# The routing steps of a fused attention, expert and SiLU kernel: the gates placed by hand, the compaction ahead of the numbers' table, pair 1's windows copied by VectorE

## The chip, the cores and the metric

The program runs on one core of a Trainium2 chip. The core has five engines with instruction streams of their own: TensorE (PE, matrix products; PEld is its weight load), VectorE (DVE), ScalarE (ACT), GpSimd (POOL) and SyncE (SP, which here only issues DMAs). Each takes its stream in order and waits on semaphores for the others. The metric is the device time of one execution in microseconds.

## The reference

Three stages follow each other on 3072 tokens of 512 numbers, all in fp32:

```python
# chunked attention: per chunk of 32 queries, 8 memory keys and a window of 56 keys
a = softmax(scale * q_c @ concat(mem_k, k_ctx).T);  x[c] = a @ concat(mem_v, v_ctx)
# top-1 mixture of 8 experts
logits = unit(x) @ unit(expert_emb).T / tau
e = argmax(logits);  gate = softmax(logits)[e]
y = gate * (relu(x @ w1[e]) @ w2[e])
# SiLU MLP
h = y @ w_in;  out = (h * sigmoid(h)) @ w_out
```

## The kernel before

Products are made in split form: an operand is cut into a rounded part and its remainder (`split`, lines 92 to 94: ScalarE rounds, VectorE subtracts), and `three` (lines 96 to 100) adds three products.

**Attention.** 16 pairs of heads, two units each. For a unit, `scores` (line 788) multiplies queries with the windows of keys in `kbuf`, VectorE takes the maximum (797) and subtracts it (800), ScalarE exponentiates (805), TensorE turns the result (811), and `values` (823) multiplies with the values. `windows` (lines 710 to 719) lays out a pair's keys: from the loaded block `kraw` it copies 56 overlapping columns for each of 12 chunks (716, the large copy) and the 8 memory columns (717, the small copy). Head 0's go by ScalarE, head 1's by VectorE for pair 0 and by GpSimd for the others. `kbuf` holds two pairs. Ahead of its first copy GpSimd zeroes buffers and makes the routing constants (lines 278 to 292). Per block of tokens `ranks` finds each token's expert and its place among that expert's tokens.

**Experts.** Tokens are gathered into slots that belong to one expert each: two leading slots of 256 tokens whose experts are found early (`pre[0]`, `pre[1]`), then up to 4 slots of 384 (`threes`) and up to 17 of 256 (`twos`). Each slot has 8 steps. In `step` (f), TensorE makes the first product of part f+1 (`first_mm`, tokens by `w1`) and then the second product of part f (`second_mm`, by `w2`). Between them the two weight parts for f+2 are split (`split_w`: `w1h`, `w1l`, then `v2h`, `v2l`), and SyncE fetches part f+5. ScalarE and VectorE split the hidden part too (183, 184: `hhs`, `hls`). In the last two steps of a slot the next slot's gathered rows are turned and split (`turn`, lines 171 and 93/94: `xhl`, `xll`).

**The routing work beside it.** The place of every token is worked out while the leading slots run. It is written as generators (`places`, `gates`, `names`, `compact`) in the list `pending`. `advance` takes the next pieces of the first generator at each point where it is called. A bare `yield` ends a piece; a `yield n` also holds the list until a call behind a block of products comes, n calls later at least. `places` ends in one-hot matrices: VectorE makes `ahf` (513), GpSimd and ScalarE scale it into `ah` (517, 518), and TensorE multiplies four groups of six (506) into the table of rows; `meta` makes the counts. `names` turns the table and stores it in `td` (546 to 550), `compact` makes for each output row the place where it lies (`rows_i`, lines 555 to 572), and `gates` makes the softmax weight of each token and stores it in `gd` (580 to 601). What is left at the end of step 6 of `pre[1]` is forced out there (`while pending`).

Of the kernel before, what the change touches and what calls it, by code (L numbers as in the profile page):

```python
# [13 lines left out]
I32 = mybir.dt.int32  # L14
# [8 lines left out]
P = 128  # L23
# [25 lines left out]
NA = 2 * N2  # L49
# [10 lines left out]
def tile_chunk_attention_top1_moe_silu_mlp(ctx, tc, qT, kT, vW, emb, tau, wm, wo, out, dbg=None):  # L60
    nc = tc.nc
    wo = wo.bitcast(I32)
    PE, ACT, DVE, POOL, SP = nc.tensor, nc.scalar, nc.vector, nc.gpsimd, nc.sync
# [10 lines left out]
    bank = [psum.tile([P, DM], F32, name=f"bank{i}") for i in range(8)]  # L74
# [33 lines left out]
    rp = rt.enter_context(tc.tile_pool(name="rp", bufs=1))  # L108
# [87 lines left out]
    def put(at, y, nt):  # L196
# [3 lines left out]
    pre = [  # L200
        Slot(2, 4, None, chosen_i[0:1, n:n + 1], lambda c, n=n: pre_i[:, 2 * n + c:2 * n + c + 1], lambda n=n: later.get("chosen", 0) > n)
        for n in range(2)
    ]
# [58 lines left out]
    shift = rp.tile([P, 1], F32, name="shift")  # L262
    lens, skip, cends, cfirst = (rp.tile([P, 2, NE], F32, name=n) for n in ("lens", "skip", "cends", "cfirst"))
    wideh = rp.tile([P, NTC, 2 * NE], F32, name="wideh")
    ahf = rp.tile([P, NT, NA], BF16, name="ahf")
    ah = rp.tile([P, NT, 2, NA], BF16, name="ah")
    ixs = rp.tile([P, NA + 3 * N3], F32, name="ixs")
# [213 lines left out]
    def places(home):  # L481

        yield from slots()
        sl = slice(LEAD, NT)
        DVE.tensor_scalar(two[:, sl], mv[:, sl, 0], e2, None, op0=ALU.is_equal)
        DVE.tensor_scalar(too[:, sl], mv[:, sl, 0], e3, None, op0=ALU.is_equal)
        yield
        DVE.tensor_tensor(two, two, too, op=ALU.add)
        part = [P, 3, NE, NT]
        DVE.tensor_tensor(hotf, hot.unsqueeze(1).to_broadcast(part), look.to_broadcast(part), op=ALU.mult)  # L490
        yield
        DVE.tensor_reduce(found, hotf.rearrange("p n e t -> p n t e"), axis=AX.X, op=ALU.add)
        yield
        DVE.tensor_tensor(found[:, 0], found[:, 0], ab[:, 0], op=ALU.is_gt)
        DVE.scalar_tensor_tensor(two, two, float(SLOT), ab[:, 0], op0=ALU.mult, op1=ALU.is_gt)
        yield
        DVE.tensor_tensor(found[:, 2], found[:, 2], found[:, 0], op=ALU.mult)
        DVE.tensor_tensor(ab[:, 0], ab[:, 0], found[:, 1], op=ALU.add)
        yield
        DVE.tensor_tensor(ab[:, 0], ab[:, 0], found[:, 2], op=ALU.add)  # L500
        yield
        DVE.scalar_tensor_tensor(ab[:, 0], two, -float(4 * N), ab[:, 0], op0=ALU.mult, op1=ALU.add)
        yield
        def products(c):
            for t in range(c * TPB, (c + 1) * TPB):
                PE.matmul(ix, lhsT=bh[:, t], rhs=ah[:, t], start=t == 0, stop=t == NT - 1)

        tables = meta()
        ix = home[:, 0:2 * NA].rearrange("p (r a) -> p r a", r=2)
        for c in range(NT // TPB):  # L510
            sl = slice(c * TPB, (c + 1) * TPB)
            part = [P, TPB, NA]
            DVE.tensor_tensor(
                ahf[:, sl], ab[:, 0, sl].unsqueeze(2).to_broadcast(part), tiles.to_broadcast(part), op=ALU.is_equal
            )
            yield
            POOL.tensor_tensor(ah[:, sl, 1], ahf[:, sl], count[:, sl].unsqueeze(2).to_broadcast(part), op=ALU.mult)
            ACT.activation(ah[:, sl, 0], ahf[:, sl], AF.Copy, scale=row)
            yield
            if c:  # L520
                yield 0
                products(c - 1)
        yield from tables
        yield LASTW
        products(c)
        yield
        DVE.tensor_scalar(ixp, ix[:, 1], float(P), None, op0=ALU.mult)
        DVE.tensor_scalar(here, countf[:, 0:N3 + 1], ends3[:, NE - 1:], None, op0=ALU.is_equal)
        yield
        DVE.tensor_tensor(ixs[:, 0:NA], ixp, ix[:, 0], op=ALU.add)  # L530
        yield
        DVE.tensor_copy(rows3_i, ixs[:, 0:3 * (N3 + 1)])
        later["placed"] = True
        flush()
        DVE.tensor_scalar(ixp, ixs[:, 0:NA], here[:, 0:1], None, op0=ALU.mult)
        yield
        for k in range(1, N3 + 1):
            out_ = rows2_i if k == N3 else ixp
            DVE.scalar_tensor_tensor(out_, ixs[:, 3 * k:3 * k + NA], here[:, k:k + 1], ixp, op0=ALU.mult, op1=ALU.add)
            yield  # L540

    def names():

        yield HOLD
        by_tile = bank[7][0:NA, 0:P]
        PE.transpose(by_tile, ixs[:, 0:NA], ident)
        yield
        names_t = wideh.rearrange("p t e -> p (t e)")[0:NA, 0:P].bitcast(I32)
        DVE.tensor_copy(names_t, by_tile)
        SP.dma_start(out=td.rearrange("(t p) o -> t (p o)", p=P), in_=names_t)  # L550
        yield

    def compact():

        DVE.tensor_tensor(lens[:, 0], rem, wide, op=ALU.min)
        yield
        DVE.tensor_tensor(lens[:, 1], rem, lens[:, 0], op=ALU.subtract)
        yield
        flat16 = lambda t: t.rearrange("p a e -> p (a e)")
        yield from starts(flat16(cfirst), flat16(lens), flat16(cends))  # L560
        DVE.tensor_tensor(skip[:, 0], row3, cfirst[:, 0], op=ALU.subtract)
        DVE.tensor_tensor(skip[:, 1], row2, cfirst[:, 1], op=ALU.subtract)
        yield
        part = [P, NTC, 2 * NE]
        across = lambda t: flat16(t).unsqueeze(1).to_broadcast(part)
        DVE.tensor_tensor(wideh, token[:, 0:NTC].to_broadcast(part), across(cfirst), op=ALU.is_ge)
        yield
        DVE.tensor_tensor(wideh, wideh, across(skip), op=ALU.mult)
        yield
        DVE.tensor_reduce(st[:, 0:NTC], wideh, axis=AX.X, op=ALU.max)  # L570
        yield
        DVE.tensor_tensor(rows_i, st[:, 0:NTC, 0], token[:, 0:NTC, 0], op=ALU.add)
        yield

    def gates():
        norm = ss.unsqueeze(2)
        while squares:
            yield
        yield HOLD
        ACT.activation(ss, ss, AF.Sqrt)  # L580
        yield HOLD
        DVE.tensor_scalar(ss, ss, 1e-6, None, op0=ALU.add)
        yield
        DVE.reciprocal(ss, ss)
        yield
        DVE.tensor_tensor(d, d, norm.to_broadcast(full), op=ALU.mult)
        yield HOLD
        ACT.activation(d, d, AF.Exp)
        yield HOLD
        DVE.tensor_reduce(gate, d, axis=AX.X, op=ALU.add)  # L590
        yield
        DVE.tensor_scalar(gate, gate, 1e-9, None, op0=ALU.add)
        yield
        DVE.reciprocal(gate, gate)
        yield HOLD
        by_tile = bank[7][0:NT, 0:P]
        PE.transpose(by_tile, gate, ident)
        yield
        gate_t = flat(seg)[0:NT, 0:P]
        DVE.tensor_copy(gate_t, by_tile)  # L600
        SP.dma_start(out=gd.rearrange("(t p) o -> t (p o)", p=P), in_=gate_t)
        yield

    pending = []
# [20 lines left out]
    duty, tail, early, mid = (defaultdict(list) for _ in range(4))  # L625
# [44 lines left out]
    def step(s, f):  # L670
        ahead_of(s, f)
        firsts(s, f)
        seconds(s, f)

    SPOTS, HOLD, RATE, LASTW, GP = (2, 6), 2, 2, 1, 2
# [7 lines left out]
    with ExitStack() as a:  # L683
# [26 lines left out]
        def windows(j, h, part):  # L710
            rows = slice(h * D, h * D + D)
            half = slice(part * (NCH // 2), (part + 1) * (NCH // 2))
            src, dst = kraw[j][rows], kbuf[j % 2][rows, h, half]
            copy = (POOL.tensor_copy if j else DVE.tensor_copy) if h else ACT.copy
            w = src[:, NMEM + half.start * CH:]
            copy(dst[:, :, NMEM:], bass.AP(tensor=w.tensor, offset=w.offset, ap=[w.ap[0], [CH, NCH // 2], [1, WIN]]))
            (POOL.tensor_copy if j > 2 else copy)(
                dst[:, :, 0:NMEM], src[:, 0:NMEM].unsqueeze(1).to_broadcast([D, NCH // 2, NMEM])
            )
# [233 lines left out]
        for i in range(1, NF - 2):  # L953
            ahead_of(pre[0], i)
            firsts(pre[0], i)
            if i == 1:
                logits2(NU - 1)
                pending.extend([places(bank[6]), gates(), names(), compact()])
            seconds(pre[0], i)
            for b, t in squares[:2]:  # L960
                square(b, t)
            del squares[:2]
# [21 lines left out]
        tail[key].append(lambda at=at: put(at, yfirst[0], 2))  # L984
    step(pre[0], NF - 2)
    step(pre[0], NF - 1)
    for f in range(NF):
        step(pre[1], f)
        if f == NF - 2:
            while pending:  # L990
                advance(pe=True)
# [320 lines left out]
```

## Time and profile before

| | |
|---|---|
| three runs | 1022.92, 1024.77, 1028.66 us; median 1024.77 |
| the profiled execution | 1027.44 us, its span 1025.7 us |
| granted TensorE clock, mean | 0.992 of full speed |
| TensorE busy | 978.3 us, 95% of the span |
| VectorE busy | 596.8 us, 58% |
| ScalarE busy | 462.5 us, 45% |
| GpSimd busy | 188.8 us, 18% |

The profile comes from one execution. Busy shares are means over the three stages: attention runs up to about 110 us, the leading slots to about 172, the other expert slots to about 470, and the SiLU MLP behind them. In a row with a bracket, the bracket gives the time that the engine stood idle ahead of the instruction and what released it.

### The profile page before, as it was taken

How to read it: one execution, taken by the hardware profiler on the slowest of the kernel's cores; microseconds unless marked ns; L12 is line 12 of the kernel's file. 1: busy time of each engine (PE TensorE's matmuls, PEld its weight loads, DVE VectorE, ACT ScalarE, POOL GpSimd, SP SyncE). 2: the span in 40 equal slices, each digit the busy share in tenths (PEclk: the TensorE clock that was granted, in tenths of full speed). 3: DMA queues.
4: the chain of work that ended last, by engine and by line, in shares of the span. 5: the costliest groups of instructions: out<-in, count | busy, mean ns of one | idle time of the engine just before them, and what ended most of it. 6: DMA issues, size and time to landing. Idle time of an engine off the chain costs nothing. (4 is left out here: it accounts for less than half of the span.)

```text
span 1025.7 us, 16830 instructions
## 1 busy us (share of the span) xinstructions
PE 978.3 (95%) x6366; PEld 823.4 (80%) x6366; DVE 596.8 (58%) x1191; ACT 462.5 (45%) x890; POOL 188.8 (18%) x259
## 2 busy tenths in 40 slices
PE   5988888999999999998999999999999999999997
PEld 4766677999888999997778888878887888788886
DVE  6778797677777888896899932422332232223221
ACT  7877655445467665663544423222321331233221
POOL 8355133011020000013130002140032005001001
PEclk9999999999999999999999999999999999999999
DMA  7987756566487887776242201020010002000001
GB/s 271 350 317 261 258 190 226 173 219 222 131 272 265 280 274 257 263 248 186 84 137 95 76 1 42 21 62 1 1 58 25 1 1 83 1 1 24 18 1 42
DMA packets 44212, 139.36 MB, mean 136 GB/s; under 512 B 6422, under 2 KB 6480, under 8 KB 44120
## 3 DMA queue, kind: packets, MB, share of 16 engines
q1 hardware_dynamic: 36632, 118.22, 33.6%
q0 software_dynamic: 7488, 19.95, 6.4%
q8 instruction: 53, 0.87, 0.3%
q14 instruction: 39, 0.32, 0.1%
HBM read 115.32 MB, written 22.84 MB: 135 GB/s over the span
## 5 line engine op out<-in xcount | busy, mean ns | idle before, releaser
L1174 DVE TENSOR_TENSOR sg<-bank,sg 128x512 f32<-128x512 f32 x96 | 66.3, 690 | 235.5 <-ACT sg L1169 230.0
L1169 ACT ACTIVATE sg<-bank 128x512 f32<-128x512 f32 x96 | 57.4, 598 | 272.4 <-PE bank L100 262.0
L98 PE MATMUL bank<-yh,w2bh 128*128 128x512 f32 x240 | 94.3, 393 | 0.0
L94 DVE TENSOR_TENSOR gl<-sg,gh 128x512 fp32r<-128x512 f32 x92 | 63.8, 693 | 51.8 <-ACT gh L93 48.1
L100 PE MATMUL bank<-yh,w2bl 128*128 128x512 f32 x240 | 93.6, 390 | 0.0
L99 PE MATMUL bank<-yl,w2bh 128*128 128x512 f32 x240 | 93.5, 390 | 0.0
L1197 POOL DMA_INDIRECT out_dram<-o,tok x20 | 20.2, 1008 | 387.9 <-DVE o L1194 347.8
L100 PE MATMUL bank<-w2bh,gl 128*128 128x512 f32 x224 | 87.4, 390 | 0.0
L98 PE MATMUL bank<-w2bh,gh 128*128 128x512 f32 x224 | 87.2, 389 | 0.0
L93 ACT CAST gh<-sg 128x512 fp32r<-128x512 f32 x92 | 57.0, 620 | 66.9 <-DVE sg L1174 64.6
L99 PE MATMUL bank<-w2bl,gh 128*128 128x512 f32 x224 | 87.2, 389 | 0.0
L183 ACT ACTIVATE hhl<-bank 128x256 fp32r<-128x256 f32 (+1 forms) x88 | 36.4, 413 | 99.3 <-PE bank L100 94.2
L98 PE MATMUL bank<-v2h,hhl 128*128 128x512 f32 x200 | 80.3, 401 | 0.0
L100 PE MATMUL bank<-v2h,hll 128*128 128x512 f32 x200 | 78.8, 394 | 0.0
L99 PE MATMUL bank<-v2l,hhl 128*128 128x512 f32 x200 | 78.3, 392 | 0.0
L94 DVE TENSOR_TENSOR w1l<-raw,w1h 128x512 fp32r<-128x512 f32 x106 | 72.9, 688 | 8.6 <-ACT w1h L93 4.9
L149 POOL DMA_INDIRECT xrowl<-xd,rows_i x28 | 30.9, 1103 | 241.4 <-PE bank L171 199.8
L94 DVE TENSOR_TENSOR v2l<-raw,v2h 128x512 fp32r<-128x512 f32 x106 | 73.0, 689 | 0.0
L184 DVE SCALAR_TENSOR_TENSOR hll<-bank,hhl 128x256 fp32r<-128x256 f32 (+1 forms) x88 | 40.4, 459 | 52.6 <-ACT hhl L183 51.1
L99 PE MATMUL bank<-xll,w1h 128*128 128x256 f32 (+1 forms) x224 | 68.7, 306 | 2.2 <-DVE xll L94 2.2
L98 PE MATMUL bank<-xhl,w1h 128*128 128x256 f32 (+1 forms) x224 | 68.9, 307 | 1.4 <-DVEq L1139 1.4
L100 PE MATMUL bank<-xhl,w1l 128*128 128x256 f32 (+1 forms) x224 | 68.7, 306 | 0.2 <-DVE w1l L94 0.2
(309 smaller groups left out, 2433.9 us busy)
## 6 DMA issues: line engine op xcount, KB each, us to landing
raw<-in_wm_dram SPq DMA_DIRECT2D x109, 512.0 KB
coded<-in_wo_dram SPq DMA_DIRECT2D x36, 512.0 KB
vbuf<-in_vW_dram SPq DMA_DIRECT2D x32, 390.0 KB
k<-in_kT_dram SPq DMA_DIRECT2D x16, 400.0 KB
q<-in_qT_dram SPq DMA_DIRECT2D x16, 384.0 KB
xd<-xb SPq DMA_DIRECT2D x8, 768.0 KB
ys<-ymore SPq DMA_DIRECT2D x8, 512.0 KB
ys<-yfirst SPq DMA_DIRECT2D x7, 512.0 KB
```

The source lines that it names most:

```text
L93: ACT.copy(hi, src)
L94: eng.tensor_tensor(lo, src, hi.bitcast(F32), op=ALU.subtract)
L98: PE.matmul(out, lhsT=lh, rhs=rh, start=start, stop=False)
L99: PE.matmul(out, lhsT=lh, rhs=rl, start=False, stop=False)
L100: PE.matmul(out, lhsT=ll, rhs=rh, start=False, stop=stop)
L149: POOL.indirect_dma_start(out=s.where["row"][:, c], out_offset=None, in_=xd[0:LEAD * P] if s in pre else xd, in_offset=IndirectOffsetOnAxi ...
L183: ACT.activation(hh, h, AF.Relu)
L184: DVE.scalar_tensor_tensor(hl, h, 0.0, hh.bitcast(F32), op0=ALU.max, op1=ALU.subtract)
L1169: ACT.activation(sg, h, AF.Sigmoid)
L1174: DVE.tensor_tensor(sg, h, sg, op=ALU.mult)
L1197: POOL.indirect_dma_start(out=out, out_offset=IndirectOffsetOnAxis(ap=tok_i[g][:, c:c + 1], axis=0), in_=o, in_offset=None,)
```

## The change

It has four parts. `gates` leaves the list `pending`; a helper `share` runs it up to its next hold, and five such calls are hung at the end of steps 0 to 4 of `pre[1]`. `compact` stands ahead of `names` in the list. `names` gets a tile of its own, `names_t`, where it used the memory of `wideh`, which `compact` fills. The first group of one-hot products is held for one more call (`yield 1`). And pair 1's windows of head 1 are copied by VectorE.

```diff
--- before.py
+++ after.py
@@ -262,6 +262,7 @@
     shift = rp.tile([P, 1], F32, name="shift")
     lens, skip, cends, cfirst = (rp.tile([P, 2, NE], F32, name=n) for n in ("lens", "skip", "cends", "cfirst"))
     wideh = rp.tile([P, NTC, 2 * NE], F32, name="wideh")
+    names_t = rp.tile([NA, P], I32, name="names_t")
     ahf = rp.tile([P, NT, NA], BF16, name="ahf")
     ah = rp.tile([P, NT, 2, NA], BF16, name="ah")
     ixs = rp.tile([P, NA + 3 * N3], F32, name="ixs")
@@ -518,7 +519,7 @@
             ACT.activation(ah[:, sl, 0], ahf[:, sl], AF.Copy, scale=row)
             yield
             if c:
-                yield 0
+                yield 1
                 products(c - 1)
         yield from tables
         yield LASTW
@@ -545,7 +546,6 @@
         by_tile = bank[7][0:NA, 0:P]
         PE.transpose(by_tile, ixs[:, 0:NA], ident)
         yield
-        names_t = wideh.rearrange("p t e -> p (t e)")[0:NA, 0:P].bitcast(I32)
         DVE.tensor_copy(names_t, by_tile)
         SP.dma_start(out=td.rearrange("(t p) o -> t (p o)", p=P), in_=names_t)
         yield
@@ -574,9 +574,6 @@
 
     def gates():
         norm = ss.unsqueeze(2)
-        while squares:
-            yield
-        yield HOLD
         ACT.activation(ss, ss, AF.Sqrt)
         yield HOLD
         DVE.tensor_scalar(ss, ss, 1e-6, None, op0=ALU.add)
@@ -711,7 +708,7 @@
             rows = slice(h * D, h * D + D)
             half = slice(part * (NCH // 2), (part + 1) * (NCH // 2))
             src, dst = kraw[j][rows], kbuf[j % 2][rows, h, half]
-            copy = (POOL.tensor_copy if j else DVE.tensor_copy) if h else ACT.copy
+            copy = (POOL.tensor_copy if j > 1 else DVE.tensor_copy) if h else ACT.copy
             w = src[:, NMEM + half.start * CH:]
             copy(dst[:, :, NMEM:], bass.AP(tensor=w.tensor, offset=w.offset, ap=[w.ap[0], [CH, NCH // 2], [1, WIN]]))
             (POOL.tensor_copy if j > 2 else copy)(
@@ -955,7 +952,7 @@
             firsts(pre[0], i)
             if i == 1:
                 logits2(NU - 1)
-                pending.extend([places(bank[6]), gates(), names(), compact()])
+                pending.extend([places(bank[6]), compact(), names()])
             seconds(pre[0], i)
             for b, t in squares[:2]:
                 square(b, t)
@@ -984,6 +981,15 @@
         tail[key].append(lambda at=at: put(at, yfirst[0], 2))
     step(pre[0], NF - 2)
     step(pre[0], NF - 1)
+    assert not squares
+    shares = gates()
+
+    def share():
+        while next(shares, HOLD) is None:
+            pass
+
+    for f in range(5):
+        tail[pre[1], f].append(share)
     for f in range(NF):
         step(pre[1], f)
         if f == NF - 2:
```

On VectorE at the start, before: the maxima and subtractions of units 0 and 1, and then the expert norms.

```order
L797 TENSOR_REDUCE mx_277<-bank_69 128x6
L800 TENSOR_TENSOR e_279<-bank_69,mx_277 128x3x2x64
L797 TENSOR_REDUCE mx_298<-bank_70 128x6
L800 TENSOR_TENSOR e_300<-bank_70,mx_298 128x3x2x64
L728 TENSOR_SCALAR en_209<-en_209 8x1
L729 TENSOR_TENSOR en_209<-en_209 8x1
L730 RECIPROCAL en_209<-en_209 8x1
L731 TENSOR_SCALAR e_208<-e_208,en_209 8x512
L797 TENSOR_REDUCE mx_334<-bank_69 128x6
```

And of the change, with the four copies in between:

```order
L794 TENSOR_REDUCE mx_278<-bank_69 128x6
L797 TENSOR_TENSOR e_280<-bank_69,mx_278 128x3x2x64
L713 COPY kbuf_205<-k_223 64x12x56
L714 COPY kbuf_205<-k_223 64x12x8
L794 TENSOR_REDUCE mx_299<-bank_70 128x6
L797 TENSOR_TENSOR e_301<-bank_70,mx_299 128x3x2x64
L725 TENSOR_SCALAR en_210<-en_210 8x1
L726 TENSOR_TENSOR en_210<-en_210 8x1
L727 RECIPROCAL en_210<-en_210 8x1
L728 TENSOR_SCALAR e_209<-e_209,en_210 8x512
L713 COPY kbuf_205<-k_223 64x12x56
L714 COPY kbuf_205<-k_223 64x12x8
```

The first pair of copies stands ahead of unit 1's maximum, the second ahead of unit 2's.

On VectorE in `pre[1]`, before, from the last piece of `places` on (539, the rows of the slots of 256); the first `w1l` behind it is the split for part 5:

```order
L539 SCALAR_TENSOR_TENSOR ixp<-ixs,here,ixp 128x34 x3
L539 SCALAR_TENSOR_TENSOR rows_i<-ixs,here,ixp 128x34
L94 TENSOR_TENSOR w1l_106<-raw_100,w1h_105 128x512
L94 TENSOR_TENSOR v2l_112<-raw_100,v2h_111 128x512
L184 SCALAR_TENSOR_TENSOR hls_116<-bank_71,hhs_115 128x256
```

And of the change:

```order
L540 SCALAR_TENSOR_TENSOR rows_i<-ixs,here,ixp 128x34
L555 TENSOR_TENSOR lens<-rem,wide 128x8
L557 TENSOR_TENSOR lens<-rem,lens 128x8
L403 SCALAR_TENSOR_TENSOR cends<-lens,countf 128x16
L405 TENSOR_TENSOR cfirst<-cends,lens 128x16
L561 TENSOR_TENSOR skip<-row_167,cfirst 128x8
L562 TENSOR_TENSOR skip<-row_168,cfirst 128x8
L566 TENSOR_TENSOR wideh<-token,cfirst 128x320
L568 TENSOR_TENSOR wideh<-wideh,skip 128x320
L570 TENSOR_REDUCE st<-wideh 128x20
L94 TENSOR_TENSOR w1l_106<-raw_100,w1h_105 128x512
L94 TENSOR_TENSOR v2l_112<-raw_100,v2h_111 128x512
```

Nine operations of the compaction now stand ahead of that `w1l`. Three of the gate's (`ss`, its reciprocal and `d`) have moved a step further up, ahead of the fourth `ahf`.

On TensorE at the end of step 6 of `pre[1]`, before: the last second product, the two turns of small tables, and the turn of the gathered rows (171).

```order
L100 MATMUL bank_74<-v2h_107,hls_116 128x512
L597 MATMUL bank_76<-ident,gate 24x128
L546 MATMUL bank_76<-ident,ixs 34x128
L171 MATMUL bank_69<-ident,xrowl 128x128 x3
L171 MATMUL bank_70<-ident,xrowl 128x128 x3
```

And of the change, around step 4, where the two turns now stand:

```order
L100 MATMUL bank_72<-xhs,w1l_106 128x256
L547 MATMUL bank_76<-ident,ixs 34x128
L98 MATMUL bank_73<-v2h_2365,hhs_115 128x512
L99 MATMUL bank_73<-v2l_2366,hhs_115 128x512
L100 MATMUL bank_73<-v2h_2365,hls_116 128x512
L98 MATMUL bank_74<-v2h_2365,hhs_115 128x512
L99 MATMUL bank_74<-v2l_2366,hhs_115 128x512
L100 MATMUL bank_74<-v2h_2365,hls_116 128x512
L594 MATMUL bank_76<-ident,gate 24x128
```

Each turn now stands beside a second product of step 4, and nothing small is left at the end of step 6.

## Rows read from the trace of the kernel before

**Rows 1.** Timeline, start: start, length, engine, line, operation, tiles, idle before.

```profile
4.21 0.51 DVE L716 COPY kbuf<-k 64x672 f32<-64x672 f32 x1
...
4.76 1.69 DVE L716 COPY kbuf<-k 64x672 f32<-64x672 f32 x1
...
6.08 1.69 POOL L763 MEMSET kbuf<- 64x1536 f32 x1
...
6.37 1.46 DVE L717 COPY kbuf<-k 64x96 f32<-64x96 f32 x1
...
7.83 2.70 POOL L764 MEMSET vbuf<- 128x3120 f32 x1
...
8.52 0.56 DVE L800 TENSOR_TENSOR e<-bank,mx 128x384 f32<-128x384 f32 x1
...
10.68 0.90 PE L811 MATMUL bank<-ident,e 128*128 128x128 f32 x3 [1.19 <-ACT e L805]
...
11.15 0.48 DVE L731 TENSOR_SCALAR e<-e,en 8x512 f32<-8x512 f32 x1
...
12.54 0.52 ACT L805 ACTIVATE e<-e 128x384 f32<-128x384 f32 x1
...
13.28 0.33 POOL L288 TENSOR_SCALAR tiles<-countf 128x34 f32<-128x34 f32 x1
...
15.31 1.51 PE L788 MATMUL bank<-kbuf,q 128*32 128x128 f32 x24 [3.73 <-POOL kbuf L717]
...
16.88 0.56 DVE L797 TENSOR_REDUCE mx<-bank 128x6 f32<-128x384 f32 x1 [5.26 <-PE bank L788]
...
19.58 0.55 PE L811 MATMUL bank<-ident,e 128*128 128x128 f32 x3
```

**Rows 2.** Stretches: length, busy of PE, PEld, DVE, ACT, POOL, clock, DMA.

```profile
20.00:24.00 4.00, 4.00 (x93) 3.34 (x94) 3.12 (x9) 3.10 (x7) 2.26 (x6) 1.00 0.29 75
24.00:28.00 4.00, 4.00 (x88) 2.95 (x78) 3.29 (x9) 3.31 (x7) 1.22 (x3) 1.00 0.98 321
```

**Rows 3.** Timeline, the second leading slot.

```profile
149.62 0.35 PE L506 MATMUL bank<-ah,bh 128*128 128x68 bf16 x6 [1.52 <-POOL ah L517]
...
152.60 0.35 PE L506 MATMUL bank<-ah,bh 128*128 128x68 bf16 x6 [0.19 <-POOL ah L517]
...
157.41 0.69 DVE L94 TENSOR_TENSOR w1l<-raw,w1h 128x512 fp32r<-128x512 f32 x1
...
158.61 0.28 PE L100 MATMUL bank<-xhs,w1l 128*128 128x256 f32 x1
...
161.27 0.17 DVE L582 TENSOR_SCALAR ss<-ss 128x24 f32<-128x24 f32 x1
...
162.09 0.69 DVE L94 TENSOR_TENSOR w1l<-raw,w1h 128x512 fp32r<-128x512 f32 x1
...
168.62 0.28 PE L597 MATMUL bank<-ident,gate 128*24 128x128 f32 x1 [1.13 <-DVE gate L594]
...
169.27 0.28 PE L546 MATMUL bank<-ident,ixs 128*34 128x128 f32 x1 [0.37 <-DVE seg L600]
...
169.80 0.15 DVE L555 TENSOR_TENSOR lens<-rem,wide 128x8 f32<-128x8 f32 x1
...
171.58 0.49 DVE L566 TENSOR_TENSOR wideh<-token,cfirst 128x320 f32<-128x320 f32 x1 [0.71 <-DMA td<-wideh]
...
173.16 0.18 DVE L572 TENSOR_TENSOR rows_i<-st,token 128x20 int32<-128x20 f32 x1
...
175.06 0.44 PE L99 MATMUL bank<-xll,w1h 128*128 128x384 f32 x1 [2.25 <-DVE xll L94]
```

**Rows 4.** Stretches behind two waits of TensorE.

```profile
175.70:179.15 3.45, 3.45 (x12) 3.45 (x12) 2.18 (x4) 1.51 (x3) 2.75 (x3) 0.51 0.94 322
876.60:880.00 3.40, 3.40 (x14) 2.51 (x15) 1.96 (x3) 1.06 (x2) 0.00 (x0) 1.00 0.00 0
```

**Rows 5.** Timeline, one wait in the SiLU MLP.

```profile
876.60 0.50 PE L98 MATMUL bank<-w2ah,gh 128*128 128x512 f32 x1 [2.23 <-ACT gh L93]
```

## The prediction

> **What bounds the kernel now.** I read the page's slices first: TensorE is busy almost throughout after the first slice, so time comes out only where it stands or runs slowly. Next the list of waits, and then the timeline of the two places that the edits touch.
>
> At the start TensorE ends three transposes at 11.58 and stands 3.73 until GpSimd has copied pair 1's second-head windows [rows 1]. GpSimd comes to that copy only behind a memset that ends at 10.53 and fifteen constants. VectorE, which now takes those copies, stands 5.26 ahead of 16.88 [rows 1].
>
> In the second leading slot three waits lie at its end: 1.13 for the gate's reciprocal, 0.37 for the copy of the turned gates, and 2.25 for a split that VectorE reaches only after the compaction [rows 3]. Then the granted clock is 0.51 over 3.45 us, so 1.2 of 2.4 GHz [rows 4]: 3.45 x 0.49 = 1.7 us of work lost. The middle of the slot is VectorE's: its rows there follow each other almost without idle time, and TensorE waits 1.52 for products' operands [rows 3].
>
> **Part A, the window copies of pair 1.** GpSimd loses four copies, VectorE gets them: a large and a small one behind the first unit's subtraction, which ends at 9.08, and again behind the row-norm operations that ended at 11.63 [rows 1]. What does such a copy cost on VectorE? The rows of pair 0 give both ends: 0.51 for a large one, and 1.46 for a small and 1.69 for a large one where GpSimd was in a memset [rows 1]. The small one at 6.37 ended at 7.83, 0.06 after the memset that began at 6.08 and took 1.69. So the copy waits for the GpSimd instruction under way and then is short.
>
> The Trainium skill says the same in "SBUF — State Buffer", Who interferes with whom: the port pair that the two engines share is an exclusive lock, and the loser blocks for the whole instruction of the other. It speaks against this edit, since the copies leave GpSimd and still queue behind it; by it, with GpSimd winning each time, the first pair would land after the last constant, near 14.3, and part A would give nothing (taken up under the wall below).
>
> I take the short end, since from 10.53 the GpSimd instructions are of the size of the one at 13.28, 0.33. So: wait until 10.53, first pair done at about 11.3 (0.51 and a constant's length), the second maximum and subtraction and the norms (2.1 us of work between 9.08 and 11.63, without the pause in it) to 13.4, second pair to 14.3. ScalarE's exponential at 12.54 is met. TensorE's third block of scores starts at 11.6 instead of 15.31. Its maximum on VectorE starts at 14.3 instead of 16.88; with two operations of 0.56 and one exponential of 0.52 the next transposes can start at 16.0. TensorE itself would be there at 11.58 + (19.58 - 15.31) = 15.9. Before it was 19.58. Gain 3.5; I take 3.4, with 3.7 (the whole wait) above. Below: four copies at 1.46 and 1.69 are 6.3, so 9.08 + 6.3 + 2.1 = 17.5 for a maximum that began at 16.88: 0.6 to 0.7 lost. GpSimd's next copies come earlier by what it no longer does, less what it is blocked; they are wanted some 3 us after that.
>
> Does the gain travel? The DMA engines are at 0.29 between 20 and 24 and at 0.98 from 24 to 28 [rows 2]. TensorE shows no wait for a load here, and loads are issued when buffers come free, so they start earlier with the compute. I carry it whole.
>
> **Part B, the second leading slot.** In step f TensorE makes the first product f+1, then the second product f; VectorE's split for first product f+2 stands between.
> - `yield 1`: the first group of one-hot products falls behind the second product of step 1. The 1.52 goes there, but all four groups now stand together and the last, at 152.60 before, waits for its `ahf`, now behind three gate operations (161.27 to 162.09: 0.82). Step 3 starts 0.3 to 0.8 late. Nothing is gained.
> - VectorE ahead of `w1l` for step 5's product: the 0.82, and the compaction up to its reduction, 169.80 to 173.16 less the 0.71 wait for the table's DMA, which its own tile `names_t` removes: 2.65. Together 3.47. That `w1l` was ready at 157.41 + 0.69 = 158.10 and TensorE's use began at 158.61: 0.5 of cover. So TensorE's third multiplication of first product 5 moves to about 161.6: **2.96 late**.
> - Behind that VectorE catches up: a step needs two splits of 0.69 and one half-split, well under a step of TensorE (about 2.8), so the gate's reduction and reciprocal and the two copies out of PSUM are covered. Without that cover they are some 1.3.
> - At the end 1.13, 0.37 and 2.25 go, and the slow stretch behind the last, 1.7: **5.45**. Next late there is the split of the first half of the gathered rows; I cost it at 0.2 or less.
> - ScalarE's two table loads move into steps where it waits for TensorE: nothing, unless the 0.5 of cover is already gone, which part B's 2.96 has in it.
> - SP: `td`, a spare store and `gd` now stand ahead of two weight fetches. `td` waits for a copy at about 165.2, so the first of these fetches goes out near 166.5, 2 us after its buffer is free; by this walk it is cast at about 173. 6 us of room: nothing. On GpSimd the gathers stay in order.
>
> B is 5.45 - 2.96 = 2.5. **Sum**: 3.4 + 2.5 = 5.9. The profiled execution took 1027.44 with a span of 1025.7, so 1021.5 for it; it was 2.7 above the median, 1024.77, from which I count: **1018.9**.
>
> **Rivals.**
> 1. *The clock falls elsewhere.* The new order leaves TensorE almost idle while it waits for four groups (some 3 us around 151), and then up to 2.5 us before 161.6. The 2.25 wait at 175.06 was followed by 1.2 GHz [rows 3, 4]; the 2.23 wait at 876.60 was not, 1.00 in the stretch behind it [rows 4, 5]. If it falls around 151, TensorE only reaches 161.6 with less waiting: free. If it falls behind 161.6, 1.7 is lost: B is 0.8, sum 4.2, 1020.6. By "TensorE: Matmul & The Clock Gate" of the Trainium skill, HAM oscillation, work in bursts between waits pays for the fall each time. The trace agrees for one of the two waits shown.
> 2. *Loads eat part A.* For: 0.98 [rows 2], so an earlier TensorE may meet k, q and v on their way. Against: the idle 20 to 24, and no wait of TensorE for them. Then A is near 0 and 2.5 stays: 1022.3. That the copies simply bring nothing, because GpSimd wins the port, ends at the same time.
> 3. *VectorE is the wall at both places.* One mechanism: what is moved onto it costs what the crowded rows say. Copies at 1.46 and 1.69: A is -0.7. In the slot TensorE waits twice for over 2 us and the clock falls twice: 5.45 - 2.96 - 3.4 = -0.9. Slower by 1.6: 1026.4. It decides where the four copies take over 5.5 us, and where both waits end in a slow stretch. Against: GpSimd's instructions after 10.53 are short, and a fall at the first wait shortens the second.
>
> **How the numbers follow.** Forecast 0.57, rival 1 0.23, rival 2 0.13, rival 3 0.07. 0.5% is 5.1 us and about what a measurement of this kernel can tell from no change; the three runs lie 5.7 apart. The forecast's 5.9 is just above that bound, so with 1 or 2 us of scatter I count two thirds of it as faster, and a third of rival 1, with a little of rival 2 through B's upper end: 0.50. Slower: half of rival 3 and a trace of scatter, 0.05. The rest, 0.45, within. If nothing of B's 2.96 came, 3.7 + 5.45 would give 1015.6; the upper end takes in rivals 1 and 2 with scatter: 1015.3 to 1023.0.
>
> **What would show it.** Right: third scores near 11.6, the waits of 1.13, 0.37 and 2.25 gone, a new wait of TensorE for `w1l` in step 5, no slow stretch at the start of the three-tile slots. Wrong: third scores after 14 (port), TensorE waiting for k, q or v after 20 (loads), no wait in step 5 (then the gain is nearer 9), or waits on both sides of it with two slow stretches.

## The result and the profile after

The changed kernel took **1016.38 us** (median of 5 runs, 1013.2 to 1018.18) against 1025.56 for the kernel before on the same chip (5 runs, 1022.92 to 1028.66): ratio 0.991, 95% interval 0.9894 to 0.9926, so 9.2 us faster. The forecast was 5.9 faster, 1018.9. Its profiled span is 1016.5 at a clock of 0.993. The names of the tiles are those of before; line numbers are 3 lower for the attention, 1 higher for the products and 6 higher for the SiLU MLP.

The timeline of the start (columns as in [rows 1]):

```profile
7.83 2.70 POOL L761 MEMSET vbuf<- 128x3120 f32 x1
...
9.14 1.75 DVE L713 COPY kbuf<-k 64x672 f32<-64x672 f32 x1
...
10.49 0.55 POOL L279 IOTA count_i<- 128x128 int32 x1
...
10.81 0.28 DVE L714 COPY kbuf<-k 64x96 f32<-64x96 f32 x1
...
11.54 1.51 PE L785 MATMUL bank<-kbuf,q 128*32 128x128 f32 x24
...
13.32 0.51 DVE L713 COPY kbuf<-k 64x672 f32<-64x672 f32 x1
...
13.74 0.22 DVE L714 COPY kbuf<-k 64x96 f32<-64x96 f32 x1
...
13.99 0.56 DVE L794 TENSOR_REDUCE mx<-bank 128x6 f32<-128x384 f32 x1
...
16.25 0.55 PE L808 MATMUL bank<-ident,e 128*128 128x128 f32 x3
```

The third scores start at 11.54 without a bracket, where 15.31 with 3.73 stood [rows 1]; the transposes behind them come at 16.25 instead of 19.58. VectorE's first copy is long (1.75): it began in the memset of 7.83 to 10.53 and ended 0.36 behind it, as in [rows 1]. The second takes 0.51 between short GpSimd instructions. GpSimd's `iota` at 10.49, beside the first copy, takes 0.55; before, without a copy of VectorE beside it, it took 0.24:

```profile
10.49 0.24 POOL L278 IOTA count_i<- 128x128 int32 x1
```

The timeline of the second leading slot:

```profile
145.23 0.84 PE L507 MATMUL bank<-ah,bh 128*128 128x68 bf16 x12 [1.48 <-POOL ah L518]
...
146.88 0.35 PE L507 MATMUL bank<-ah,bh 128*128 128x68 bf16 x6 [0.81 <-POOL ah L518]
...
153.73 0.48 DVE L570 TENSOR_REDUCE st<-wideh 128x20 f32<-128x320 f32 x1
...
154.13 0.68 DVE L94 TENSOR_TENSOR w1l<-raw,w1h 128x512 fp32r<-128x512 f32 x1
...
154.87 0.39 PE L100 MATMUL bank<-xhs,w1l 128*128 128x256 f32 x1 [1.75 <-DVE w1l L94]
...
158.37 0.28 PE L594 MATMUL bank<-ident,gate 128*24 128x128 f32 x1 [0.58 <-DVE names_t L549]
```

The forecast wait for `w1l` is there, right behind the compaction's reduction. No TensorE wait of 0.5 us or more follows up to 180: the 1.13, the 0.37 and the 2.25 of [rows 3] are gone. The stretch at the start of the three-tile slots, which had a clock of 0.51 [rows 4], has 1.00 (the number after the five engines' busy times):

```profile
166.77:170.20 3.43, 3.43 (x21) 3.43 (x20) 1.43 (x4) 1.24 (x4) 2.76 (x2) 1.00 1.01 343
```

The same TensorE instruction can be looked up in both traces. A shift, here and below, is its start in the one less its start in the other. The start moved by -3.5 us behind the third scores, by a further -2.6 from the first to the last step of the slot, and by -2.8 near 876, where the wait of [rows 5] is missing. The rest up to the spans' 9.2 goes both ways: before had a TensorE wait of 1.99 marked "issue" at 56.23 and a slow stretch behind it that after has not, after has two, of 1.08 at 76.32 and 1.01 at 485.27, and slow stretches elsewhere.

### The profile page after: what moved, and what is told of

It is laid out like the page before. It is cut to its first block, busy times and chain, and to the rows that moved or that the text cites. A ratio compares the mean times of both kernels' runs of the same rounds, so it can differ in the third digit from the quotient of the medians.

```text
span 1016.5 us, 16830 instructions
## 1 busy us (share of the span) xinstructions
PE 975.5 (96%) x6366; PEld 822.6 (81%) x6366; DVE 599.4 (59%) x1195; ACT 461.8 (45%) x890; POOL 187.4 (18%) x255
```

## Experiments

The runs fell on several chips, of two kinds. On the first kind the kernel before takes about 1025 us, as in the first result; on the second about 1008. Theory 1 was that the two edited places add up (3.5 and 2.5) and the rest is chance; theory 2 that the earlier start, or the new order, also spares waits elsewhere; theory 3 that the slot is worth 5 to 6, more than its profile shows.

**Both parts apart, on the second kind of chip.** `a_only` is the kernel before with this edit alone, `b_only` the changed kernel without it; `after_again` and `before_again` are the two kernels unchanged.

```diff
-            copy = (POOL.tensor_copy if j else DVE.tensor_copy) if h else ACT.copy
+            copy = (POOL.tensor_copy if j > 1 else DVE.tensor_copy) if h else ACT.copy
```

> Only the copies of pair 1's windows go to VectorE; the routing steps stand as before. Theory 1 (the two edits add, and the rest of the measured 9.2 us is stalls elsewhere that come and go between executions): third block of scores near 11.5 us, 3.5 us gained by 24 us, median 3 to 4 us below the kernel before. Theory 2 (the earlier start also spares TensorE the stall of 1.99 us near 56 us and the slow stretch behind it, in every execution): median 6 to 7 below. Theory 3 (the leading slot is worth more than the profiles show): 3 to 4 here, and 5 to 6 in the run with part B alone.

> The gates by hand, the compaction ahead of the names, names_t and yield 1, but pair 1's copies on GpSimd as before. Theory 1: median 2.5 us below the kernel before (waits of 1.13, 0.37 and 2.25 and the slow stretch gone at the slot's end, a new wait of 1.5 to 2.5 in step 5); third scores at 15.3. Theory 2: the same 2.5. Theory 3: 5 to 6.

> The changed kernel once more, to see how much of the 9.2 us repeats and which waits outside the edited places come back. Theory 1: 6 to 9 us below the kernel before, with TensorE waits for its own instructions (marked issue) at other places than in the first profile or of other length. Theory 2: again 9, with no wait of 2 us before 100 us. Theory 3: again 9, whatever waits stand before 100 us.

> The kernel before, profiled once more. Theory 1: the wait of 1.99 us near 56 us need not come again, or comes elsewhere. Theory 2: it comes again near 56 us, with the slow stretch behind it. Theory 3 says nothing of it.

Against 1008.39 (17 runs): A alone 1005.45, ratio 0.9971 (0.9958 to 0.9984); B alone 1007.45, 0.9994 (0.9985 to 1.0003), no measurable change; both 1003.68, 0.9953 (0.9939 to 0.9966). So -2.9, -0.9 and -4.7: the two parts' 3.8 and the 4.7 agree within the intervals. All three are less than was expected: 4.7 where every theory asked for 6 or more, 0.9 where theory 1 asked for 2.5 and theory 3, which falls, for 5 to 6. At their places the profiles show what they show on the first chip: against `before_again` what stands behind the third scores is 2.8 to 3.3 earlier by 24 us, and the slot gains 2.5 with part B. Why the medians show less than these two together isn't shown. `before_again` (1007.94) has no waits near 690, 783 and 876, which make 11 of the 17 us between the two kinds, and none at 56.

In `after_again` the slot shows a fall of the clock. Its TensorE timeline:

```profile
144.24 0.84 PE L507 MATMUL bank<-ah,bh 128*128 128x68 bf16 x12 [1.48 <-POOL ah L518]
...
145.89 0.35 PE L507 MATMUL bank<-ah,bh 128*128 128x68 bf16 x6 [0.81 <-POOL ah L518]
...
153.88 0.39 PE L100 MATMUL bank<-xhs,w1l 128*128 128x256 f32 x1 [0.18 <-DVE w1l L94]
```

and the stretch behind the four groups:

```profile
146.70:150.11 3.41, 3.41 (x14) 3.03 (x13) 3.27 (x17) 1.58 (x3) 1.21 (x1) 0.51 0.02 6
```

At 1.2 GHz some 1.7 us of TensorE's work are lost there, and the wait for `w1l` falls from 1.75 to 0.18. This is what the prediction's first rival called free: VectorE's row of work decides when step 5 goes on, and TensorE reaches it slowly or waits. The slot's gain is 2.5 with the fall and 2.6 in the first profile, which has none:

```profile
145.60:149.00 3.40, 2.47 (x26) 2.38 (x26) 3.26 (x22) 1.67 (x4) 0.59 (x2) 1.00 0.47 172
```

A fall behind the four groups is in five of the seven profiles that have these two waits: `after_again`, `after_third`, `names_first`, `b_only` and `b_only_2`. In `copies_all` it stands behind the wait for `w1l` instead (1.81, then 0.56 from 162.8 to 166.2), and `after` has none.

**The order inside the slot, on the first kind.** `after_third` is the changed kernel. `names_first` puts the compaction back behind the table, `yield0` takes back the later first group:

```diff
-                pending.extend([places(bank[6]), compact(), names()])
+                pending.extend([places(bank[6]), names(), compact()])
```

```diff
-                yield 1
+                yield 0
```

`spread` moves the groups into step 2, the gathers a step later and the compaction to the ends of steps 3 to 5:

```diff
-            if c:
-                yield 1
-                products(c - 1)
+        yield 1
+        for c in range(NT // TPB):
+            products(c)
         yield from tables
-        yield LASTW
-        products(c)
...
-    SPOTS, HOLD, RATE, LASTW, GP = (2, 6), 2, 2, 1, 2
+    SPOTS, HOLD, RATE, LASTW, GP = (2, 6), 2, 2, 1, 3
...
-                pending.extend([places(bank[6]), compact(), names()])
+                pending.extend([places(bank[6]), names()])
...
-    for f in range(5):
+    for f in (0, 2, 3, 4, 5):
         tail[pre[1], f].append(share)
+    packing = compact()
+    for f, n in ((3, 2), (4, 6), (5, 9)):
+        tail[pre[1], f].append(lambda n=n: [next(packing, None) for _ in range(n)])
```

> The changed kernel once more, as the measure for the other three. Sum of the two edited places (theory 1: A 3.5, B 2.5, each seen in the profiles at its place): 4 to 6 us below the kernel before. Rival (the edits also spare TensorE waits elsewhere, as the first pair of medians, 9.2 apart, would have it): 8 to 10 us below.

> The changed kernel with names() ahead of compact() as before; the gates stay by hand. Theory 1 (VectorE's backlog of routing work in the middle of the second leading slot is what TensorE meets, in whatever order it stands): the wait for w1l in step 5 (0.2 to 1.8 in the two profiles) goes, one of about the same size comes a step later, where the compaction (2.65 us) then stands ahead of a split; within 1 us of the changed kernel. Rival (compacting ahead of the table is what part B's gain comes from): 2 us or more slower than the changed kernel, with a wait near 2.2 for xll at the end of the slot again.

> The changed kernel with `yield 0` ahead of the first group of products, as before. Theory 1 (nothing is gained by `yield 1`): the wait of 1.5 for ah in step 2 comes back ahead of the second product, those of 1.48 and 0.81 behind it shrink to about 0.3 each, the end of step 4 is where it was; within 1 us of the changed kernel. Rival (the four groups together make the clock fall behind them, 1.7 us lost, seen at 146.7 in one profile of the changed kernel and not in another): the granted clock stays at full speed between 140 and 155 and the kernel is 1 to 2 us faster.

> The changed kernel with the routing work spread: all four groups of one-hot products behind the first product of step 2, where their operands are long ready; the gathers a step later; the gates' steps at the ends of steps 0, 2, 3, 4, 5; the compaction in three pieces at the ends of steps 3, 4, 5. Theory 1 (in steps 2 to 4 TensorE waits for VectorE's backlog, behind step 5 VectorE has idle time): the waits of 1.48 and 0.81 and the 0.58 for the gates' turn go, those for w1l stay under 0.5 each, and without them no slow stretch: 2 to 4 us below the changed kernel. Rival (the amount of VectorE's work is the limit, not where it stands): the waits reappear at w1l or hls of steps 3 to 5; within 1 us of the changed kernel.

| | median us | ratio to before, 1024.65 (11 runs) | shift over the slot, against the profile before |
|---|---|---|---|
| after_third | 1014.59 | 0.991 (0.9895 to 0.9925) | -2.2 |
| names_first | 1015.45 | 0.9913 (0.9896 to 0.993) | -2.5 |
| yield0 | 1016.41 | 0.9919 (0.9902 to 0.9935) | -1.5 |
| spread | 1013.9 | 0.9901 (0.9886 to 0.9917) | -3.7 |

The medians of the four can't be told apart (expected were 2 to 4 below the changed kernel for `spread`, which came out 0.7 below, and within 1 us of it for `yield0`, 1.8 above). So 10 us below before came again: theory 1's 4 to 6 is too small on this kind of chip.

In `names_first` the `w1l` wait is gone and TensorE waits a step later, at the gate's turn, about as theory 1 said. The rival that part B lives on compacting ahead of the table falls: no wait for `xll` came back. What `names_first` keeps of part B is mainly the gates placed by hand, so these are what is left to carry it; no run puts the gates alone back.

```profile
157.01 0.28 PE L594 MATMUL bank<-ident,gate 128*24 128x128 f32 x1 [0.97 <-DVE gate L591]
```

In `yield0` the 1.52 came back, the groups' waits shrank as expected, and the fall of the clock did not go: it moved behind a longer wait at step 5. Its TensorE timeline, and the stretch behind that wait:

```profile
142.23 0.35 PE L507 MATMUL bank<-ah,bh 128*128 128x68 bf16 x6 [1.52 <-POOL ah L518]
...
154.00 0.58 PE L100 MATMUL bank<-xhs,w1l 128*128 128x256 f32 x1 [1.98 <-DVE w1l L94]
```

```profile
154.60:158.05 3.45, 3.45 (x15) 3.10 (x15) 2.86 (x9) 1.41 (x3) 0.00 (x0) 0.60 0.59 189
```

Here the fall is paid, for nothing behind step 5 waits for VectorE: 1.5 in the slot instead of 2.2. That is the mechanism of the prediction's rival 1, a fall behind the `w1l` wait, brought about by taking `yield 1` back; `copies_all` has it too, with 1.7.

In `spread` the groups hardly wait, the clock stays at 1.00 through the slot, and two waits for `w1l` remain (the rival's point: VectorE's amount of work still counts). Its profile gains 1.1 to 1.5 more in the slot; the median, 0.7 lower, does not show it.

```profile
145.44 0.35 PE L507 MATMUL bank<-ah,bh 128*128 128x68 bf16 x6 [0.39 <-POOL ah L518]
...
152.57 0.39 PE L100 MATMUL bank<-xhs,w1l 128*128 128x256 f32 x1 [1.17 <-DVE w1l L94]
...
159.73 0.38 PE L100 MATMUL bank<-xhs,w1l 128*128 128x256 f32 x1 [1.11 <-DVE w1l L94]
```

**Which part carries the 10 us.** `before_third`, `a_only_2` and `b_only_2` repeat kernels from above; they fell on a chip of the first kind. `copies_all` lets VectorE make head 1's large copies of every pair (`j > 99` for `j > 1`); the small ones of pairs 3 to 15 stay on GpSimd, where they were before too.

> The kernel before once more, for a profile. Two chips so far, told apart by the kernel before: about 1025 and about 1008. On the first its one profile has two things that none of the profiles of the changed kernel has: a wait of TensorE marked issue at 56 us with a slow stretch behind it (3.2 us together) and a ScalarE wait marked issue of 3.46 at 863.6, followed by TensorE's 2.23 at 876.6 (2.8 us). Theory 1 (such waits fall differently in each execution): on a chip of the first kind at least one of them is absent now. Theory 2 (they belong to the kernel before, on that chip): both are there again. On a chip of the second kind neither is, by either theory.

> The kernel before with part A alone, again. On the second kind of chip -2.9 us, as measured. On the first kind, theory 1 (the 9.2 us there are A 3.5, B 2.5 and stalls elsewhere that either part can shift): -3 to -7. Theory 2 (A's earlier start spares the stall at 56 us): -6 to -7, with no issue wait at 56; and the wait near 876 still there if part B removes it.

> The changed kernel without part A, again. On the second kind of chip -1 us, as measured. On the first kind, theory 1: -2 to -5. Theory 2 (part B's changed order spares the ScalarE wait at 863 and so TensorE's 2.8 us near 876): -5 to -6, with the stall at 56 still there.

> The changed kernel with the second head's windows of every pair copied by VectorE, not those of pairs 0 and 1 alone. In the stretch from 36 to 68 us VectorE is busy 26.0 of 32.0 us and GpSimd's 22 large copies of 0.75 and the small ones beside them are 1.3 us of a pair's 6.1. Theory (rival 3's mechanism: VectorE has no room there): 11 half-pairs' large copies at 0.51 to 0.75 are 11 to 17 us more on VectorE, whose idle time between 20 and 95 us is about 14: 2 to 10 us slower than the changed kernel. Rival (the idle time takes them, and GpSimd's copies no longer block the port): within 1 us.

Against 1023.9 (23 runs): `a_only_2` 1017.08, ratio 0.9929 (0.9912 to 0.9946); `b_only_2` 1022.04, 0.9983 (0.9965 to 1.0001); `copies_all` 1026.1, 1.0021 (1.0005 to 1.0037). Part A alone is worth 6.8 here and 2.9 on the other kind; part B 1.9 and 0.9, neither of which can be told from nothing.

`before_third` (1025.54) has no wait at 56, so that stall is chance, as theory 1 said, and theory 2's reason for A falls. It does have the wait near 876. ScalarE, GpSimd and TensorE there, in `before_third`:

```profile
854.24 0.97 POOL L1197 DMA_INDIRECT out_dram<-o,tok  x1 [2.54 <-DMA out_dram<-o,tok]
...
856.38 0.60 ACT L1169 ACTIVATE sg<-bank 128x512 f32<-128x512 f32 x1 [3.46 <-PE bank L100]
...
861.82 0.60 ACT L1169 ACTIVATE sg<-bank 128x512 f32<-128x512 f32 x1 [3.46 <-issue]
...
869.39 0.94 POOL L1072 DMA_INDIRECT gt<-gd,tok  x1 [0.30 <-issue]
...
872.69 0.60 ACT L1169 ACTIVATE sg<-bank 128x512 f32<-128x512 f32 x1 [8.90 <-PE bank L100]
...
874.71 0.50 PE L98 MATMUL bank<-w2ah,gh 128*128 128x512 f32 x1 [2.12 <-ACT gh L93]
```

ScalarE's sigmoids follow each other every 5.44 us; the one due at 867.26 comes at 872.69. Behind GpSimd's last scatter of a group (`out_dram`, 854.24) stand twelve gathers, the last of which ends at 870.33; the held sigmoid starts 2.36 later. A wait on TensorE is not what held it, although the bracket names TensorE: the product that it takes ended more than 5 us earlier. The same rows in `a_only_2`:

```profile
845.39 0.97 POOL L1197 DMA_INDIRECT out_dram<-o,tok  x1 [2.93 <-DMA out_dram<-o,tok]
...
847.14 0.60 ACT L1169 ACTIVATE sg<-bank 128x512 f32<-128x512 f32 x1 [3.46 <-PE bank L100]
...
852.58 0.60 ACT L1169 ACTIVATE sg<-bank 128x512 f32<-128x512 f32 x1 [3.46 <-PE bank L100]
...
858.02 0.60 ACT L1169 ACTIVATE sg<-bank 128x512 f32<-128x512 f32 x1 [3.46 <-PE bank L100]
...
861.85 0.95 POOL L1072 DMA_INDIRECT gt<-gd,tok  x1 [0.30 <-issue]
...
864.01 0.60 ACT L1169 ACTIVATE sg<-bank 128x512 f32<-128x512 f32 x1 [4.01 <-PE bank L100]
```

The scatter stands 0.4 later (2.93 behind the one before, not 2.54), so the sigmoids are due 1.75, 7.19 and 12.63 behind it, not 2.14, 7.58 and 13.02. The third gets through; the fourth is 0.55 late, and TensorE doesn't wait. Read from that scatter, the held sigmoid starts at 18.41 to 18.79 in all ten profiles on this kind of chip, and the one ahead of it is due at 12.55 to 12.63 in the six with part A as the change has it (all get through) and at 13.02 to 13.04 in `before`, `before_third`, `b_only_2` and `copies_all` (none does). On the second kind nothing is held: 13.03 and 18.47 run as due. So the 2.8 us come with part A, by 0.4 us of phase between GpSimd and ScalarE. What holds the sigmoid, the traces don't show. Why the scatter is 0.4 later can be followed one step. These are the DMA queues (packets, MB, share of the 16 engines) in the idle time ahead of the scatter, first in `before_third` (851.70 to 854.24), then in `a_only_2` (842.46 to 845.39):

```profile
q0 software_dynamic: 80, 0.26, 27.1%
```

```profile
q0 software_dynamic: 80, 0.26, 24.0%
q14 instruction: 1, 0.01, 0.7%
```

The same 80 packets move, and in `a_only_2` one transfer of an instruction queue beside them. One starts 1.37 to 1.41 ahead of the scatter in all eight profiles where that idle time is 2.92 to 2.99 (two of them on the second kind); in the six others, at 2.52 to 2.54, none falls into it. `copies_all` aside, the transfer comes when VectorE has run 1126 to 1129 of its instructions and GpSimd 234 to 246, so it seems to go with VectorE's stream, which part A makes four copies longer. That a shorter stream of GpSimd suffices is excluded by `copies_all`, which has still fewer copies on GpSimd and the old phase; there no such transfer falls within 50 us ahead of the scatter. That the transfer is what delays the scatter is inferred, since no run moves it alone.

`copies_all` also settles how far part A carries. Its stretches, then its copies on VectorE between 20 and 84 us:

```profile
36.00:52.00 16.00, 13.98 (x290) 10.89 (x290) 14.32 (x40) 12.73 (x31) 3.32 (x10) 1.00 0.98 344
52.00:68.00 16.00, 14.26 (x295) 10.84 (x293) 14.30 (x41) 11.81 (x27) 5.68 (x12) 1.00 0.87 301
```

```profile
L713 DVE COPY kbuf<-k 64x672 f32<-64x672 f32 x21 | 10.9, 519 | 0.6
```

and the same stretches of `after_third`:

```profile
36.00:52.00 16.00, 14.97 (x336) 11.73 (x329) 13.00 (x41) 13.93 (x35) 6.09 (x15) 1.00 1.00 373
52.00:68.00 16.00, 15.16 (x319) 11.65 (x323) 12.97 (x38) 12.99 (x30) 10.01 (x22) 1.00 1.00 369
```

VectorE goes from 26.0 to 28.6 of 32 us busy, and TensorE from 30.1 to 28.2: by 100 us the kernel is 8 behind `after_third`. With the wait of 876 back it ends 11.5 above it (two chips, medians), beyond the 2 to 10 expected: rival 3's wall, which four copies at the start don't meet and thirty more do.

## Why the prediction was right, and its size too small

- **Part A at its place: right.** 3.4 forecast. The third scores start at 11.54 in eight of the nine profiles with part A (forecast 11.6; 13.19 in `spread`, whose first scores came 1.4 late), and what follows is 3.0 to 4.0 earlier by 20 us in these eight. The row of steps held too: first pair done at 11.09 (11.3), second maximum work to 13.3 (13.4), second pair at 13.96 (14.3), transposes at 16.25 (16.0). The lock came as the Trainium skill has it ("SBUF — State Buffer", Who interferes with whom): 1.75 for a copy that began in a memset; in `spread` a small one that did took 2.78, where a free one took 0.22, and the second unit's scores waited for it. But that GpSimd wins each time, as the prediction took the page for this rival, did not come: the `iota` of 0.55 beside the first copy shows GpSimd held as well, and behind 10.53 VectorE's copies came through at once.
- **Part A carried whole, and no further: here the sum failed on the first kind of chip.** The sum took the median and subtracted what two edited places give. [rows 5] was read for the clock alone, so its wait stood in the sum at nothing, without a reason; that 2.23 belonged to a hold of ScalarE during GpSimd's gathers, and the edit shifted the two against each other. With this 2.8 the sum is 3.5 + 2.5 + 2.8 = 8.8, and 9.2 was measured. That 1016.38 still lies in the range is luck: its lower end, 1015.3, was worked out for the case that nothing of B's 2.96 came, and all of it came. The prediction named a gain nearer 9 as the sign of no wait in step 5; it came with that wait. On the second kind, where ScalarE isn't held, 4.7 was measured, under the forecast's 5.9. Rival 2 had part A eaten by loads: 0.5 to 0.8 of it went between 20 and 50 us in three profiles (`a_only`, `after_third`, `names_first`), but the kernel before differs from itself by as much there (`before_third` is 0.8 behind `before` by 20 us and 2.0 by 50).
- **Part B: right in sum, both terms too small, and that they cancel is luck.** Forecast 5.45 removed and 2.96 late. Measured in the first pair: late 3.6 (0.5 by step 3, about 2.1 at the `w1l` wait, about 0.9 with the gates' turn, which the prediction held covered by VectorE catching up), removed 6.1 to 6.2, net 2.6. Some 0.6 on both sides are the two small turns themselves (0.28 each), which only moved. The net is 2.2 to 2.6 in five profiles with the whole of part B, 1.7 in `copies_all`. These are readings of profiles: the medians of part B alone don't show it.
- **`yield 1`: right that nothing is gained, for a reason only half seen.** Step 3 was 0.5 late, as forecast. `yield0` shows what it does: it puts the stand of TensorE, and the fall of the clock where there is one, ahead of step 5, where VectorE covers it.
- **The clock.** Waits of 1.48 and 0.81 together were followed by a fall in five of seven profiles, and not in the first one of the changed kernel (1.00 from 145.6 to 149.0). "TensorE: Matmul & The Clock Gate" of the Trainium skill, HAM oscillation, describes a matmul kernel whose bursts between waits paid for the fall each time; the traces agree in these five. So rival 1's first half, a fall in front of the `w1l` wait, is what usually came, and it was free or nearly so, as the prediction said.

## What to carry to other kernels

A gain at one place adds to one at another when each is walked through its own waits; but measure each part alone, on more than one chip, before the sum is believed. Four copies moved from one engine's stream to another's can shift a wait 800 us later, so a wait whose chain holds one of the two engines belongs among the terms. Move work onto a crowded engine only where its own row shows a hole as long as the work, and put a wait that can't be removed ahead of another that covers it.

## What the runs showed of the hardware

- On chips of one kind only, a sigmoid of ScalarE can start up to 5.4 us late while GpSimd issues gathers one behind the other (0.95 us each, 0.30 between): near 860 us those due 12.6 us or less behind the last scatter came on time, and the next one, due at 13.0 or at 18.0 to 18.1, came at 18.4 to 18.8 in ten profiles.
- The idle time ahead of that scatter was 2.92 to 2.99 in the eight profiles with an 8 KB transfer of an instruction queue in it, and 2.52 to 2.54 in the six without.
- The same kernel takes 1025 on one kind of chip and 1008 on the other; of the difference 11 us are the three places near 690, 783 and 876 (4.4, 4.1 and 2.8).
- A large copy takes 0.52 on VectorE (519 ns in `copies_all`) and 0.75 on GpSimd (748 ns in `after_third`); it is still GpSimd that should have it, where VectorE has no hole.
